# w1 groups in two transfers of 256 KB, a reserve for each transpose in the plan, and a newly drawn order

## The chip, the cores and the metric

The kernel runs on one core of one Trainium2 chip. The metric is the device time of one execution in microseconds (us), the median of several. A core has the engines TensorE (PE, with its weight loads shown apart as PEld), VectorE (DVE), ScalarE (ACT), GpSimd (POOL) and SyncE (SP), which here issues nearly all transfers.

## The reference

A block of a transformer on one sequence of 2048 tokens of width 576, all in bf16. The attention works on four segments of 512 tokens, with 32 heads of 18: causal softmax attention inside a segment, and a memory `M`, `z` of all earlier segments, mixed by a gate per head. The feed-forward part has 4608 hidden units.

```python
def _A_ref(x, wq, wk, wv, wo, beta):
    ...
    phi = lambda t: jnp.where(t > 0, t + 1.0, jnp.exp(t))
    ...
    for s in range(N):                                   # 4 segments of 512
        logits = jnp.einsum('bhqd,bhkd->bhqk', qs, ks) * scale + mask
        p = _softmax(logits, axis=-1)
        a_dot = jnp.einsum('bhqk,bhkd->bhqd', p, vs)
        pq = phi(qs)
        num = jnp.einsum('bhld,bhde->bhle', pq, M)
        den = jnp.einsum('bhld,bhd->bhl', pq, z)[..., None] + 1e-06
        o = g * (num / den) + (1.0 - g) * a_dot
        outs.append(o)
        pk = phi(ks)
        M = M + jnp.einsum('bhld,bhle->bhde', pk, vs)
        z = z + jnp.einsum('bhld->bhd', pk)
    ...
    return o @ wo

def _B_ref(x, w1, b1, w2, b2):
    h = jnp.einsum('bsd,df->bsf', x, w1) + b1
    h = _gelu(h)
    return jnp.einsum('bsf,fd->bsd', h, w2) + b2

h = x + _A_ref(_layernorm(x), A_wq, A_wk, A_wv, A_wo, A_beta)
h2 = h + _B_ref(_layernorm(h), B_w1, B_b1, B_w2, B_b2)
```

## The kernel before

The 2048 tokens are worked on in 8 chunks of 256 (16 tiles of 128). Every chunk goes through these streams:

- **stream_P**: layernorm, the normed tile transposed (`xT`), the projections to q, k and v (L551 and L552, in `mm5`), q and k transposed into `QT` and `KT`. The first chunks transpose on TensorE (L582, L670), the later ones by a DMA transpose (`dma_t`, L323).
- **stream_A**: 80 visits of scores (L752, sixteen small matmuls in tiles of 32 rows, four at a time into `st`), the exponential on ScalarE (L758), the causal mask on GpSimd or VectorE (L763, L765), and the weighted values (L784, into `ox`). From the second segment on, the memory's part (L794 to L814) is added.
- **stream_M**: the memory's sums (L710) for six chunks.
- **stream_B**: the attention's output transposed (by `dma_t` from the second chunk on), the output projection, residual, second layernorm, and its transpose `xn2T`.
- **stream_F1**: the first feed-forward product in 9 groups of 512 hidden units for each chunk, 72 groups in all. Each group needs a fresh copy of its part of w1, in one of up to eight buffers (two of their own, `w1g`, three that lie in `hT` for a while, three in `wqkv` once the projections are done). The width 576 is cut into 4 x 128 rows (`w1_main`, L1061) and 64 left over, the tails. From the second chunk on the tails run as matmuls in tiles of 64 rows (L1048) ahead of the group's others; behind the attention's end up to three groups share one such stretch. The bias is added by VectorE (L1071) or ScalarE (L1069), the gelu by ScalarE (L1083).
- **stream_F2**: the second product (L1110), 36 matmuls for each half of a tile, then the residual from `hd` by way of `hc` (L1099) and the store (L1118, L1120).

The order of all this is not left to the program's text. The kernel contains a planner that plays the execution through with fixed costs: each `op` has an engine, a duration, what it reads and writes, and a due time, which is the plan's clock plus an entry of `SLACK`; `PHASES` replaces entries of `SLACK` at certain times of the plan. Whenever an engine is free, the ready operation with the earliest due time goes first. TensorE takes what the streams offer, with rules for joining a stretch of scores with a stretch of tails (`linger`, `alone`). Where nothing is ready in the beginning, it creates a filler, a matmul on zeros (L1179). A transfer has a `receipt` time beside its bytes (`transfer`, `begin`); its landing frees what waits for it in the plan.

When the plan is done, `arranged` takes each engine's operations in the order of the plan and moves some of them: `MOVES` is a table of pairs for each engine, "operation number i behind operation number j". The numbers are places in the list `ops`, in the order of creation. The result is issued as it stands, each engine in its own order; semaphores hold the data dependencies on the chip. So a plan that errs shows as waits, and the order is not adapted on the chip.

All transfers go through SP's one queue, in the order of the table. Those that the change touches are made in `load_w1` (L974 the main part of 512 KB, L977 twice 32 KB for the tails) and in `dma_t` (L323).

Of the kernel before, what the change touches and what calls it, by code (L numbers as in the profile page):

```python
# [16 lines left out]
def kernel(  # L17
# [16 lines left out]
    P = 128  # L34
# [24 lines left out]
    def sbuf(name, shape, dt=BF16):  # L59
# [8 lines left out]
    NEVER = 1e9  # L68
    TABLE_LOAD = 1.283
    SLACK = dict(zero=19, head=36, lnp=38.5, lnb=53, pow=-202, apply=-44.5, ek_k=497.5, relu_k=102, min_k=61, add_k=34.5,  # L70
                 mz=152.5, exp=-105.5, ek=-79.5, relu=-88.5, min=192.5, add=160, hb=-200.5, gelu=56, finish=35.5, mem=-80,
                 sum=23.5, out=-77.5, hd=122.5, xp=-148, xb=-22.5, t_x=-121.5, t_q=365, t_k=36, t_o=175.5, t_h=161, w1=101,
                 w2=116.5, hc=-15, evict=-236.5, qk=-22.5, ot=126.5, mask=78.5, lead=42.5, balance=254, alone=0, linger=1.5,
                 g=9.5, x1=80, hold=-133.5, ln0=-100)
# [11 lines left out]
                        t_q=338.5, t_h=201, w1=161.5, hc=156.5, qk=-90, ot=27, lead=41.25, balance=118.5, g=90, x1=13, hold=-201.5)),  # L86
              (90, dict(zero=-3, head=133, lnp=103, lnb=42.5, pow=-287, apply=-65.5, ek_k=456, relu_k=25, min_k=-34, add_k=73.5,
# [7 lines left out]
                        balance=117.5, g=86.5, x1=31, hold=-200.5)),  # L95
              (130, dict(lnp=38, lnb=63.5, relu_k=119, min_k=-28, add_k=105, mz=66.5, min=116, add=113.5, gelu=21, finish=17,
# [16 lines left out]
              (240, dict(zero=-55, head=-105.5, lnp=36.5, lnb=91.5, pow=-253.5, apply=23, ek_k=666.5, relu_k=262, min_k=-78.5,  # L113
                        add_k=59, mz=-61.5, exp=2.5, ek=6, relu=-109, min=204.5, add=-49.5, hb=-348, gelu=3.5, finish=3, mem=-13,
                        sum=179, out=-151.5, hd=101.5, xp=-381.5, xb=-36.5, t_x=-116.5, t_q=343.5, t_k=282.5, t_o=180, t_h=235,
                        w1=95.5, w2=120, hc=194.5, evict=-454, qk=-86.5, ot=26, mask=-34, lead=36, balance=190.5, linger=2.5, g=213,
                        x1=34.5, hold=-86.5, ln0=42)),
# [7 lines left out]
              (330, dict(zero=-20, head=-128.5, lnp=11.5, lnb=94.5, pow=-248.5, apply=-19, ek_k=787.5, relu_k=313, min_k=-113.5,  # L125
                        add_k=84.5, mz=-51, exp=74, ek=-71, relu=-139, min=71, add=-38.5, hb=-398.5, gelu=-87, finish=-8.5,
                        mem=-44.5, sum=155.5, out=-124.5, hd=207.5, xp=-331.5, xb=-36.5, t_x=-24.5, t_q=422.5, t_k=139.5, t_o=142,
                        t_h=382.5, w1=123, w2=70.5, hc=13.5, evict=-539.5, qk=-92.5, ot=95, mask=62, lead=34.5, balance=193,
                        alone=4, linger=1, g=359, x1=94, hold=-139, ln0=-106)),
# [7 lines left out]
    MOVES = dict(PE=[74, -1, 71, 73, 77, 71, 81, 78, 75, 81, 85, 75, 89, 80, 93, 89, 86, 82, 90, 84, 83, 88, 97, 83, 94, 97, 102,  # L137
# [30 lines left out]
                                      ACT=[59, 53, 61, 54, 45, 113, 124, 120, 135, 124, 55, 130, 155, 145, 168, 171, 224, 218, 56,  # L168
# [152 lines left out]
    def dma_t(blocks, dst, src, rd, wr, slack=0.0):  # L321

        o = op("SP", 1.25, lambda: nc.sync.dma_start_transpose(out=dst, in_=src), rd, wr, slack)  # L323
        return transfer(o, blocks * 45 + 70, 1.4, rd, wr, 0.2)
# [221 lines left out]
    def mm(n):  # L546
        return n * MM + 0.003
# [710 lines left out]
```

## Time and profile before

| | before |
|---|---|
| runs | 467.14, 467.19, 468.15 us; median 467.19 |
| profiled execution | 467.02 us, of which the span in the profile is 465.1 us |
| granted TensorE clock | 0.999 of full speed |
| busy TensorE / weight loads | 459.2 us / 351.6 us |
| busy VectorE / ScalarE / GpSimd | 272.9 / 320.0 / 180.0 us |
| DMA | 80.89 MB, mean 174 GB/s; the main queue's packets take 69.7% of the 16 DMA engines |
| issued by SP | 393 transfers, 64 of them transposes |

A view by stretches gives, for each stretch of the span, the busy time of each engine with the number of its instructions, then the granted clock and the DMA's share and rate. A row of the waits gives who waited, for whom, the sum, the number of times and the longest, in us; PEld is TensorE's weight load, SPq the queue of SP, and "issue" means that nothing in the profile released it. A timeline row gives start, length, engine, line, operation and tiles, shape and number of instructions; lengths of matmuls overlap with the next row, so starts are compared.

### The profile page before, as it was taken

What the parts mean: (1) busy time and instruction counts of PE and PEld (TensorE: products, weight loads), DVE (VectorE), ACT (ScalarE), POOL (GpSimd) and SP (SyncE); (2) the same over time, 40 slices, a digit from 0 to 9 for tenths busy, and PEclk for the clock granted to TensorE, in tenths of its full rate; (3) what the DMA queues carried; (4) which work ended last, traced back from release to release, by engine and by line L of the source; (5) the groups of instructions that cost most, each with busy time, mean ns of one, the idle gap of its engine ahead of it and who ended that gap; (6) DMA issues with size and microseconds to landing.
All of it is one profiled execution on the core that took longest, in us unless ns stands there. A gap on an engine that the chain in (4) does not pass through costs nothing.

```text
span 465.1 us, 14420 instructions
## 1 busy us (share of the span) xinstructions
PE 459.2 (99%) x6102; PEld 351.6 (76%) x6102; DVE 272.9 (59%) x712; ACT 320.0 (69%) x299; POOL 180.0 (39%) x240
## 2 busy tenths in 40 slices
PE   8999999999999999999999999999999999999997
PEld 6777787777677777767677777678778788888885
DVE  4889878787874355777755647687345524212020
ACT  3987788977888877966768778658778453423620
POOL 4567233778563144487442116474233401000000
PEclk9999999999999999999999999999999999999999
DMA  8889699887598557587876645989956595747211
GB/s 210 251 257 293 127 205 192 177 216 153 130 220 205 167 148 222 129 164 150 152 178 184 176 154 149 169 192 196 229 168 178 167 215 169 155 126 222 68 40 51
DMA packets 123152, 80.89 MB, mean 174 GB/s; under 512 B 57536, under 2 KB 121040, under 8 KB 123088
## 3 DMA queue, kind: packets, MB, share of 16 engines
q1 hardware_dynamic: 123056, 79.98, 69.7%
q8 instruction: 47, 0.77, 0.7%
q0 software_dynamic: 32, 0.01, 0.1%
q14 instruction: 17, 0.14, 0.1%
HBM read 60.03 MB, written 7.08 MB: 144 GB/s over the span
## 4 chain that ended last, share of the span: by engine, by line
PE 96%; DMA 2%; DVE 1%; SPq 0%; issue 0%
PE bank L1110 25%; PE bank L1061 22%; PE bank L551 14%; PE ox L784 7%; PE st L752 6%; PE late L1110 5%; PE late L1061 4%; PE bank L1048 4%; PE bank L552 3%; DMA wqkv<-in_A_wq_dram 2%; PE bank L1021 1%; PE ox L1110 1%; PE bank L807 1%; PE bank L670 1%; PE ox L1061 1%; PE bank L710 1%
## 5 line engine op out<-in xcount | busy, mean ns | idle before, releaser
L758 ACT ACTIVATE pt<-st 128x2048 bf16<-128x2048 f32 x80 | 150.2, 1878 | 56.8 <-PE st L752 51.5
L1110 PE MATMUL bank<-w_sb,hT 128*128 128x288 bf16 x936 | 135.9, 286 | 0.0
L1110 PEld LDWEIGHTS <-hT 128*128 128x128 bf16 x1152 | 109.1, 98 | 26.9 <-issue 1.1
L1071 DVE TENSOR_TENSOR hT<-bank,b1T 128x512 bf16<-128x512 f32 x78 | 53.8, 689 | 69.0 <-PE bank L1061 68.5
L1061 PE MATMUL bank<-xn2T,w1g 128*128 128x256 bf16 x688 | 87.9, 273 | 0.0
L1061 PEld LDWEIGHTS <-w1g 128*128 128x128 bf16 x768 | 70.6, 98 | 16.0 <-issue 6.7
L763 POOL TENSOR_SCALAR_AFFINE_SELECT pt<-pt 128x512 bf16<-128x512 bf16 x84 | 54.1, 657 | 71.2 <-ACT pt L758 66.3
L1083 ACT ACTIVATE hT<-hT 128x1536 bf16<-128x1536 bf16 (+3 forms) x24 | 66.0, 2764 | 16.4 <-DVE hT L1071 16.2
L551 PE MATMUL bank<-wqkv,xT 128*128 128x432 bf16 (+1 forms) x268 | 57.1, 336 | 0.7 <-DMA wqkv<-in_A_wq_dram 0.7
L551 PEld LDWEIGHTS <-xT 128*128 128x128 bf16 x400 | 36.5, 97 | 19.7 <-issue 0.9
L784 PEld LDWEIGHTS <-pt 128*128 128x128 bf16 x1280 | 42.2, 96 | 4.5 <-issue 0.6
L784 PE MATMUL ox<-v_aug,pt 128*128 128x19 bf16 x1280 | 44.1, 172 | 0.0
L752 PE MATMUL st<-QT,KT 32*128 32x128 bf16 x1280 | 32.4, 217 | 0.6 <-issue 0.6
L799 POOL TENSOR_TENSOR pq<-ek,pq 128x512 bf16<-128x512 bf16 x24 | 27.9, 1162 | 12.6 <-DVE ek L797 10.8
L752 PEld LDWEIGHTS <-KT 32*128 32x128 bf16 x1280 | 18.5, 92 | 16.2 <-issue 14.3
L829 POOL TENSOR_TENSOR o_nat<-t,t 128x288 bf16<-128x288 f32 x24 | 19.9, 830 | 25.7 <-DVE t L828 25.6
L1069 ACT ACTIVATE hT<-bank,b1T 128x256 bf16<-128x256 f32 x62 | 25.8, 473 | 5.6 <-PE bank L1061 4.6
L1061 PEld LDWEIGHTS <-wqkv 128*128 128x128 bf16 x272 | 26.0, 98 | 4.5 <-issue 0.4
L1110 PE MATMUL late<-w_sb,hT 128*128 128x288 bf16 x180 | 25.0, 286 | 0.0
L795 POOL TENSOR_SCALAR pq<-QT 128x512 bf16<-128x512 bf16 x24 | 15.4, 641 | 24.7 <-PE bank L807 9.9
L569 POOL TENSOR_TENSOR rstd_b<-rstd_b,mhalf 128x1 f32<-128x1 f32 x16 | 9.6, 602 | 39.2 <-DVE rstd_b L564 39.2
L931 POOL TENSOR_TENSOR h_t<-h_t,b_bc 128x576 f32<-128x576 f32 x16 | 20.7, 1296 | 6.0 <-DVE xn L573 4.8
(136 smaller groups left out, 620.1 us busy)
## 6 DMA issues: line engine op xcount, KB each, us to landing
w1g<-in_B_w_dram SPq DMA_DIRECT2D x50, 512.0 KB, 4.3
wqkv<-in_B_w_dram SPq DMA_DIRECT2D x17, 512.0 KB, 4.1
w_sb<-in_B_w_dram SPq DMA_DIRECT2D x6, 864.0 KB, 6.0
hd<-h_t SPq DMA_DIRECT2D x16, 288.0 KB, 3.0
hc<-hd SPq DMA_DIRECT2D x32, 144.0 KB, 2.8
w1g<-in_B_w_dram SPq DMA_DIRECT2D x100, 32.0 KB, 3.1
x_b<-in_A_x_dram SPq DMA_DIRECT2D x18, 144.0 KB, 3.7
hT<-in_B_w_dram SPq DMA_DIRECT2D x5, 512.0 KB, 5.6
```

The lines of the kernel that those rows point to most:

```text
L551: nc.tensor.matmul(out=out_ap, lhsT=lhsT_of(slice(0, P), k), rhs=rhs_of(slice(0, P), k), start=(k == 0), stop=False)
L752: nc.tensor.matmul(out=st4[:, i, n * P:(n + 1) * P], lhsT=KTs[(c - c % 2 + kt // 2) % 3][rows, g, (kt % 2) * P:(kt % 2 + 1) * P], rhs=QTs[ ...
L758: op("ACT", 1.88, lambda: nc.scalar.activation(out=pt[:], in_=st4[:], func=ACT.Exp, scale=scale), sk, [("pt", slot, n) for n in range(4)], ...
L763: either(("POOL", 0.64, lambda part=part: nc.gpsimd.affine_select(out=part, in_=part, pattern=[[0, 4], [1, P]], compare_op=ALU.is_ge, fill ...
L784: nc.tensor.matmul(out=oxv[:, 4 * (g % 4) + i, :], lhsT=pts[slot][:, i, n * P:(n + 1) * P], rhs=v_augs[(2 * s0 + kt) % 6][:, 4 * g + i, :] ...
L799: op("POOL", 1.16, lambda: nc.gpsimd.tensor_tensor(out=pq[:], in0=e_g, in1=pq[:], op=ALU.add), ["ek"], ["pq"], slack=SLACK["add"])
L931: op("POOL", 1.29, lambda: nc.gpsimd.tensor_tensor(out=h_t[:], in0=h_t[:], in1=b2_bc[:], op=ALU.add), ["b2"], [("h", tl)], slack=SLACK["hb"])
L1061: nc.tensor.matmul(out=banks[b][:, a * Q:(a + 1) * Q], lhsT=w1_main(wt)[:, k, (2 * (h % 2) + a) * P:(2 * (h % 2) + a + 1) * P], rhs=xn2T[c ...
L1069: nc.scalar.activation(out=hT[:, f + a, :], in_=banks[b][:, a * Q:(a + 1) * Q], func=ACT.Identity, bias=b1T[:, f + a:f + a + 1])
L1071: either(("DVE", 0.69, lambda hT=hT, f=f, b=b: nc.vector.tensor_tensor(out=hT[:, f:f + 2, :], in0=banks[b][:].rearrange("p (a w) -> p a w" ...
L1083: op("ACT", (f1 - f0) * Q * 0.00083 + 0.18, lambda hT=hT, f0=f0, f1=f1: nc.scalar.activation(out=hT[:, f0:f1, :], in_=hT[:, f0:f1, :], fun ...
L1110: nc.tensor.matmul(out=acc, lhsT=hT[:, q, tl * P:(tl + 1) * P], rhs=w2_sb[:, q, hs], start=(q == 0), stop=(q == NF - 1))
```

## The change

Four edits. (1) `load_w1` issues the 512 KB of a group as two transfers of 256 KB, each with a key of its own; the matmuls wait for both. The two transfers of 32 KB for the tails stay. (2) In the plan each transpose lands `RESERVE` = 0.6 us later than before; `d.pad` is read nowhere in the kernel. (3) The due times: the base entries of `SLACK` are replaced, two new entries of `PHASES` come in at 50 and 110 us, those at 240 and 330 us are changed in part, the others stay. (4) `MOVES` is another table (TensorE 305 pairs for 295, ScalarE 77 for 68, VectorE 265 for 287, GpSimd 113 for 112, SP 268 for 213). No computation changes.

```diff
+    RESERVE = 0.6
-    SLACK = dict(zero=19, head=36, lnp=38.5, lnb=53, pow=-202, apply=-44.5, ek_k=497.5, relu_k=102, min_k=61, add_k=34.5,
...
+    SLACK = dict(zero=25.5, head=44, lnp=45.5, lnb=75, pow=-181.5, apply=-50, ek_k=548.5, relu_k=99.5, min_k=59.5, add_k=64,
...
+              (50, dict(zero=65, head=49, lnp=67.5, lnb=42, pow=-339, apply=-21.5, ek_k=540, relu_k=61, min_k=-62, add_k=101.5,
...
+              (110, dict(head=78.5, lnp=20.5, min_k=-14.5, add_k=82, mem=-149.5, sum=113.5, out=-68.5, t_q=345.5, w1=129.5, hc=116,
...
     MOVES = dict(PE=[...],
...
-                                      SP=[7, 8, 6, 7, 65, 6, 210, 65, 318, 210, 64, 318, 190, 9, ... 189, 417,
-                      ... 2504, 2492, 2539, 2527])
+                                      SP=[3, 1, 5, 2, 72, 4, 8, 7, 66, 8, 192, 66, 215, 192, 235, 215, 71, 235, 327, 71, 194, 327,
+                      233, 194, 65, 10, 236, 65, 191, 236, 9, 191, 268, 11, 70, 63, 214, 70, 220, 214, 299, 220, 213, 299, 281, 64,
+                      193, 281, ... 2599, 2587, 2611, 2598])
...
     def dma_t(blocks, dst, src, rd, wr, slack=0.0):
 
         o = op("SP", 1.25, lambda: nc.sync.dma_start_transpose(out=dst, in_=src), rd, wr, slack)
-        return transfer(o, blocks * 45 + 70, 1.4, rd, wr, 0.2)
+        d = transfer(o, blocks * 45 + 70, 1.4, rd, wr, 0.2 + RESERVE)
+        d.pad = RESERVE
+        return d
...
-        dma(512, lambda: nc.sync.dma_start(out=w1_main(wt), in_=B_w1[0:512, fcols].rearrange("(k p) f -> p k f", p=P)), (), [k], SLACK["w1"])
+        for h in range(2):
+            dma(256, lambda h=h: nc.sync.dma_start(out=w1_main(wt)[:, 2 * h:2 * h + 2, :],
+                                                   in_=B_w1[256 * h:256 * h + 256, fcols].rearrange("(k p) f -> p k f", p=P)), (), [(*k, "m", h)], SLACK["w1"])
...
-                        wk = [k, (*k, 0), (*k, 1)]
+                        wk = [(*k, 0), (*k, 1), (*k, "m", 0), (*k, "m", 1)]
...
-                wk = [key for _, k in w1s for key in (k, (*k, 0), (*k, 1))]
+                wk = [key for _, k in w1s for key in ((*k, 0), (*k, 1), (*k, "m", 0), (*k, "m", 1))]
...
-                        op("PE", 4 * mm(Q), go, xk + [k], [b], n=8)
+                        op("PE", 4 * mm(Q), go, xk + [(*k, "m", 0), (*k, "m", 1)], [b], n=8)
```

More of the change, by code (lines that the diff above doesn't have):

```diff
@@ L68 @@
     NEVER = 1e9
+    RESERVE = 0.6
     TABLE_LOAD = 1.283
-    SLACK = dict(zero=19, head=36, lnp=38.5, lnb=53, pow=-202, apply=-44.5, ek_k=497.5, relu_k=102, min_k=61, add_k=34.5,
[L71 to L74, printed above, removed]
+    SLACK = dict(zero=25.5, head=44, lnp=45.5, lnb=75, pow=-181.5, apply=-50, ek_k=548.5, relu_k=99.5, min_k=59.5, add_k=64,
+                 mz=214, exp=-121, ek=-80, relu=-54.5, min=168.5, add=162.5, hb=-204, gelu=61.5, finish=-14.5, mem=-108.5,
+                 sum=51, out=-14.5, hd=136.5, xp=-155.5, xb=-8.5, t_x=-147.5, t_q=388.5, t_k=61.5, t_o=174, t_h=190, w1=118,
+                 w2=138, hc=-47, evict=-218.5, qk=-24, ot=127, mask=60.5, lead=41.25, balance=254, alone=0, linger=2.5,
+                 g=3.5, x1=81, hold=-179.5, ln0=-138)
     PHASES = [(30, dict(zero=31.5, head=69.5, lnp=42, pow=-174, apply=-18.5, ek_k=572, relu_k=123, min_k=-8, add_k=97, mz=106.5,
@@ L86 @@
                         t_q=338.5, t_h=201, w1=161.5, hc=156.5, qk=-90, ot=27, lead=41.25, balance=118.5, g=90, x1=13, hold=-201.5)),
+              (50, dict(zero=65, head=49, lnp=67.5, lnb=42, pow=-339, apply=-21.5, ek_k=540, relu_k=61, min_k=-62, add_k=101.5,
+                        mz=109.5, exp=-48, ek=-251, relu=-111.5, min=79.5, add=130, hb=-298, gelu=-28, finish=38, mem=-96, sum=160,
+                        out=-71.5, hd=214.5, xp=-236, xb=15, t_x=-120.5, t_q=375.5, t_k=-43, t_o=146.5, t_h=153.5, w1=145.5, w2=22,
+                        hc=191.5, evict=-362.5, qk=-130.5, ot=68.5, mask=63.5, lead=35.5, balance=104, linger=4, g=73, x1=2.5,
+                        hold=-235, ln0=46.5)),
               (90, dict(zero=-3, head=133, lnp=103, lnb=42.5, pow=-287, apply=-65.5, ek_k=456, relu_k=25, min_k=-34, add_k=73.5,
@@ L95 @@
                         balance=117.5, g=86.5, x1=31, hold=-200.5)),
+              (110, dict(head=78.5, lnp=20.5, min_k=-14.5, add_k=82, mem=-149.5, sum=113.5, out=-68.5, t_q=345.5, w1=129.5, hc=116,
+                        evict=-324, ot=38, balance=117)),
               (130, dict(lnp=38, lnb=63.5, relu_k=119, min_k=-28, add_k=105, mz=66.5, min=116, add=113.5, gelu=21, finish=17,
@@ L112 @@
                         evict=-346.5, qk=-100.5, ot=31, lead=43, balance=141, linger=1, g=138.5, x1=56.5, hold=-173, ln0=-88.5)),
[L113 to L117, printed above, removed]
+              (240, dict(zero=-55, head=-105.5, lnp=36.5, lnb=93.5, pow=-254.5, apply=31, ek_k=666.5, relu_k=264, min_k=-78.5,
+                        add_k=59, mz=-61.5, exp=2.5, ek=4, relu=-107, min=204.5, add=-49.5, hb=-348, gelu=-0.5, finish=-30, mem=-14,
+                        sum=179, out=-167.5, hd=125.5, xp=-413.5, xb=-36.5, t_x=-116.5, t_q=343.5, t_k=282.5, t_o=180, t_h=243,
+                        w1=95.5, w2=119.5, hc=194.5, evict=-454, qk=-86.5, ot=26, mask=-42, lead=37, balance=198.5, linger=2.5,
+                        g=213, x1=30.5, hold=-134.5, ln0=42)),
               (290, dict(zero=-27.5, head=-102.5, lnp=22, lnb=89.5, pow=-245, apply=-23.5, ek_k=777.5, relu_k=282, min_k=-137,
@@ L124 @@
                         hd=174.5, xp=-350.5, xb=-45.5, t_x=-47, t_q=371, t_k=169.5, qk=-84, ot=27, mask=74.5, alone=0.3, ln0=-89)),
[L125 to L129, printed above, removed]
+              (330, dict(zero=-20, head=-162.5, lnp=11.5, lnb=94.5, pow=-248.5, apply=-19, ek_k=787.5, relu_k=313, min_k=-113,
+                        add_k=52.5, mz=-51, exp=70, ek=-103, relu=-139, min=71, add=-42.5, hb=-398.5, gelu=-87, finish=-8.5,
+                        mem=-44.5, sum=155.5, out=-124.5, hd=207.5, xp=-347.5, xb=-36.5, t_x=-24.5, t_q=422.5, t_k=139.5, t_o=142,
+                        t_h=385.5, w1=123, w2=70.5, hc=-18.5, evict=-539.5, qk=-92.5, ot=95, mask=62, lead=34.5, balance=193,
+                        alone=4, linger=0, g=359, x1=95.5, hold=-124, ln0=-106)),
               (360, dict(zero=-34, lnp=5.5, lnb=93.5, pow=-238, ek_k=659, relu_k=282.5, min_k=-9, mz=-118.5, exp=-35, ek=17,
```

9 lines of the change are left out of this document (4 added, 5 removed), and 200 rows, old and new, of tables (ACT, DVE, MOVES, POOL).

## The prediction

> **What bounds the kernel now.** I read the profile's page first, then busy times by stretch, then the waits of TensorE and of its weight loads, then its timeline.
>
> ```profile
> PE 459.2 (99%) x6102; PEld 351.6 (76%) x6102; DVE 272.9 (59%) x712; ACT 320.0 (69%) x299; POOL 180.0 (39%) x240
> PE 96%; DMA 2%; DVE 1%; SPq 0%; issue 0%
> ...
> 0.00:23.00 23.00, 21.08 (x236) 16.44 (x237) 15.73 (x57) 14.88 (x22) 12.04 (x24) 1.00 0.84 229
> 23.00:90.00 67.00, 66.23 (x1163) 50.29 (x1162) 57.09 (x151) 55.76 (x45) 32.21 (x44) 1.00 0.89 214
> 90.00:372.00 282.00, 281.98 (x3915) 211.78 (x3913) 178.47 (x466) 215.35 (x189) 133.33 (x171) 1.00 0.72 174
> 372.00:462.00 90.00, 89.95 (x796) 73.05 (x793) 21.16 (x41) 34.03 (x45) 2.41 (x3) 1.00 0.51 135
> 462.00:465.20 3.20, 0.00 (x0) 0.00 (x0) 0.45 (x1) 0.00 (x0) 0.00 (x0) 0.84 0.08 23
> ```
>
> TensorE is busy 459.2 us of 465.1, and 96% of the chain that ended last is TensorE. The stretches show where the other 5.9 us are: 1.9 in the first 23 us, 0.8 up to 90 us, 0.1 in the 372 us after that, 3.2 behind the last matmul. The granted clock is 1.00 wherever matmuls run. From 90 us on no wait is left to be removed. What TensorE waited for, in total, times and the longest in us:
>
> ```profile
> PE ox L1179 <- DVE pq L508: 1.3, 1, 1.3
> PE bank L551 <- DMA wqkv<-in_A_wq_dram: 0.7, 1, 0.7
> PE st L752 <- issue: 0.6, 1, 0.6
> ...
> PEld L752 <- issue: 14.3, 55, 0.8
> PEld L1061 <- issue: 7.6, 36, 0.2
> PEld L1048 <- issue: 4.9, 20, 0.4
> ...
> PEld L551 <- DMA xT<-o_nat: 0.2, 1, 0.2
> PEld L1061 <- DMA QT<-qk_pad: 0.2, 1, 0.2
> PEld L1061 <- DMA w1g<-in_B_w_dram: 0.2, 1, 0.2
> ```
>
> Two of the three waits of the matmuls are the start of the kernel (constants, the first weights). In the whole run the weight loads waited once for a w1 transfer and twice for a transpose, 0.2 us each. These are the transfers that the change deals with, so little can come back from them. But "busy" still hides something: 14.3 + 7.6 + 4.9 = 26.8 us of "issue" before the weight loads of three lines, those where the array changes between tiles of 32 rows (scores, L752), of 64 rows (the tails of F1, L1048) and whole ones. The timeline gives the price:
>
> ```profile
> 138.75 0.55 PE L784 MATMUL ox<-v_aug,pt 128*128 128x19 bf16 x16
> 139.24 0.40 PE L752 MATMUL st<-QT,KT 32*128 32x128 bf16 x16
> 139.57 0.39 PE L1048 MATMUL bank<-xn2T,w1g 64*128 64x256 bf16 x4
> 139.90 1.05 PE L1061 MATMUL bank<-xn2T,w1g 128*128 128x256 bf16 x8
> ...
> 141.06 0.55 PE L784 MATMUL ox<-v_aug,pt 128*128 128x19 bf16 x16
> 141.46 1.03 PE L1061 MATMUL bank<-xn2T,w1g 128*128 128x256 bf16 x8
> 142.33 0.44 PE L710 MATMUL bank<-v_aug,phik_pad 128*128 128x76 bf16 x8
> 142.61 1.14 PE L1110 MATMUL bank<-w_sb,hT 128*128 128x288 bf16 x8
> 143.68 0.40 PE L752 MATMUL st<-QT,KT 32*128 32x128 bf16 x16
> ...
> L752 PEld LDWEIGHTS <-KT x1280: 90/93/94, 15.1 to 366.5; 32*128 32x128 bf16 x183
> ...
> L1048 PEld LDWEIGHTS <-w1g x192: 92/94/96, 71.5 to 436.7; 64*128 64x128 bf16 x192
> ```
>
> Sixteen matmuls of L784 take 141.46 - 141.06 = 0.40 us before whole tiles and 139.24 - 138.75 = 0.49 before scores: a change of tiling costs 0.09 us. At 139.24 scores and tails stand side by side, three changes instead of four. Counted through the whole timeline, from 15.1 to 436.7 us, there are 80 stretches of scores (1280 / 16) and 55 of tails, 40 of the 55 with a score beside them: 2 x (80 + 55) - 40 = 230 changes, about 21 us. At best all 55 are joined, which takes 15 changes away: 1.4 us.
>
> [...]
>
> **The change, part by part.** The sum is made on the profiled execution: 467.02 us, of which 465.1 are its span; the median of the three runs is 467.19, 0.17 more.
>
> ```profile
> w1g<-in_B_w_dram SPq DMA_DIRECT2D x50, 512.0 KB, 4.3
> wqkv<-in_B_w_dram SPq DMA_DIRECT2D x17, 512.0 KB, 4.1
> ...
> hd<-h_t SPq DMA_DIRECT2D x16, 288.0 KB, 3.0
> hc<-hd SPq DMA_DIRECT2D x32, 144.0 KB, 2.8
> ...
> hT<-in_B_w_dram SPq DMA_DIRECT2D x5, 512.0 KB, 5.6
> ...
> L974 SPq DMA_DIRECT2D w1g<-in_B_w_dram x50: 372/498/1672, 16.1 to 424.3; - x50
> ...
> L323 SPq DMA_TRANSPOSE xT<-o_nat x14: 1204/1212/1846, 55.3 to 372.6; - x14
> ...
> L323 SPq DMA_TRANSPOSE KT<-qk_pad x12: 1241/1276/2548, 63.7 to 329.6; - x12
> ...
> DMA to landing us min/median/max: 2.6/3.6/5.8
> ```
>
> Two transfers for one. There are 50 + 17 + 5 = 72 loads, so 72 transfers are added, at 0.5 us of SP's time each: 36 us. SP issues in order, so what stands behind a second half is 0.5 us later: often a transpose, or the two small tails of the same group. A half should land 2.8 to 3.0 us after its issue (between the rows for 144 and 288 KB), and the second half, issued 0.5 us behind the first, in 3.3 to 3.5, against 4.3 for the whole. A wait of TensorE becomes two, on transfers that land one behind the other; its price, where the data are there, is zero up to the 0.05 us of a semaphore instruction (row below), 55 times, hence 0 to 2.8 us:
>
> ```profile
> L1048 PEldq EVENT_SEMAPHORE  x7: 51/51/51, 93.5 to 407.0; - x7
> ```
>
> I take zero, since at 139.57 the tails follow 0.33 us behind scores, just as L1061 follows the tails, although they already wait for three transfers. A gain is bounded by the one 0.2 us wait.
>
> [...]
>
> The reserve. Each of the 64 transposes (14 + 14 + 12 + 12 + 12 in five groups, the first and the last of them above) counts as landed 0.6 us later in the plan; the chip does nothing more for it. Where a reader would have stood at once behind the landing, other work goes in first. Cover: other streams have matmuls ready (281.98 busy of 282.00). Without cover it would cost 64 x 0.6 = 38 us. I take zero for it, and -0.3 for what it removes: two waits of 0.2 us, less what comes up elsewhere. It also covers the 0.5 us that SP is later.
>
> Due times and moves. This is the part with no row of its own: another order of the same matmuls. The diff bounds it. The numbers in the table are places in the list of operations as the plan makes them. SP's largest goes from 2539 to 2611, by 72, just the added transfers; the first w1 load behind the start begins at 189 before, and SP's numbers 191 to 194 can only be that load after: two more operations ahead of it, those of the first two groups. So the new plan very likely has the same fillers and the same groups of tails, and TensorE's work is the same:
>
> ```profile
> L1179 PE MATMUL bank<-pq 128*128 128x256 bf16 x43 | 9.1, 338 | 0.0
> L1179 PE MATMUL ox<-pq 128*128 128x256 bf16 x10 | 3.3, 372 | 1.3 <-DVE pq L508 1.3
> ```
>
> These 53 fillers stand where nothing is ready, all in the first 23 us; their number shows how much of the start is dependence. Left to the order are the changes of tiling: 5 more or fewer (a third of the 15) make 0.45 us either way; I take 0, as nothing in the diff says which way. The 3.2 us behind the last matmul are an eviction and a store and stay.
>
> Sum: 467.0 + 0 (split) - 0.3 (waits) + 0 (order) = 466.7 for a profiled execution, and with the 0.17 above, 466.9 for the median.
>
> **The rivals.** First, the new order is shorter. All 15 joins (1.4), the 0.6 us of "issue" in L752 and the 0.3 from above make 2.3 us, 464.9; two thirds of that, 1.5, give 465.7. For it: 26.8 us of changes is the only reserve in the trace, and the due times that decide on them are all new. Against it: a gain of over 0.2% (0.93 us, about what a measurement of this kernel can tell from no change) needs some ten joins, or seven and a wait, out of fifteen.
>
> Second, slower: an order drawn up in a plan meets transfers and engines that are not where the plan has them. The place is SP's queue between 90 and 372 us. There the transposes alone hold SP for 64 x 1.2 = 77 us, the 72 w1 loads with their two small tails for 72 x 3 x 0.5 = 108, and 144 after. One load that waits for its buffer holds up all behind it:
>
> ```profile
> SPq L974 <- PE bank L1061: 22.4, 17, 3.4
> ```
>
> A transpose behind such a wait (1.3 us on average, 3.4 at most) is late by 0.5 us more than now, and TensorE, which takes its own order as written, stands until it lands. With the wait's 1.3 us, less the reserve, a stall is about 0.7 us: two make it slower, three cost 2.1 us, 469.0. For it: three transfers already land in the moment of their use (the waits of 0.2), so that the margins are near zero at places. Against it: the reserve is larger than the 0.5 us.
>
> Third, the reserve and the split do nothing, and the order comes out alike: 467.2, inside my forecast.
>
> **How the numbers follow.** No change beyond 0.2% (466.9, own range 466.3 to 468.1): 0.37, with the third rival in it. Shorter order: 0.30. Stalls: 0.33. For an 80% range I leave out 0.09 below 465.2 (nearly all joins) and 0.10 above 469.2 (more than three stalls). The range is mostly that of the stalls, whose number no row gives.
>
> **What would show it.** Right: TensorE's busy time within 1 us of 459.2, 53 fillers, the "issue" rows of L752, L1061 and L1048 together within 0.5 us of 26.8, no DMA behind a wait of PE or PEld above 0.3 us, 144 w1 transfers of 256 KB landing in 3 to 3.5 us. The first rival shows in the "issue" rows (down by over 1 us) at the same number of matmuls; the second in the stretches 90:372 and 372:462, with TensorE's busy time under 281 or 89 us and a transpose, a w1 load or a softmax tile as releaser. The forecast is wrong if the number of fillers differs, for then the start was planned anew, which I excluded, or if the time behind the last matmul does.

## The result and the profile after

The changed kernel takes 473.93 us (median of four runs, 472.12 to 476.30) against 467.44 for the kernel before beside it (467.14 to 468.15): a ratio of 1.0143 with a 95% interval of 1.0118 to 1.0168, slower by 6.7 us. The prediction said 466.9 us in 465.2 to 469.2. The profiled execution took 472.75 us, of which 471.0 are its span, 5.9 more than before.

The page of the profile after, its busy times and the chain that ended last, by engine and then by line:

```profile
PE 461.6 (98%) x6102; PEld 353.6 (75%) x6102; DVE 257.2 (55%) x689; ACT 322.4 (68%) x318; POOL 183.8 (39%) x247
PE 94%; DMA 3%; ACT 1%; DVE 0%; issue 0%; SPq 0%; ACTq 0%
```

TensorE's matmuls are the same in number, 6102, but it is busy 2.4 us longer, and DMA has gone from 2% to 3% of the chain. The view by stretches of the kernel after says where:

```profile
0.00:23.00 23.00, 21.66 (x265) 17.04 (x266) 17.68 (x62) 15.16 (x22) 12.71 (x25) 1.00 0.89 254
23.00:90.00 67.00, 65.17 (x1165) 49.91 (x1164) 54.51 (x148) 55.46 (x48) 37.18 (x53) 0.97 0.82 206
90.00:372.00 282.00, 278.89 (x3832) 208.52 (x3829) 164.52 (x440) 208.73 (x189) 130.83 (x168) 0.99 0.73 169
372.00:462.00 90.00, 90.00 (x802) 73.72 (x800) 19.56 (x38) 43.08 (x62) 3.06 (x3) 1.00 0.51 148
```

The start is a little better filled (21.66 against 21.08). Between 23 and 372 us two things are new: TensorE stands 1.8 and 3.1 us, where it stood 0.8 and 0.02, and the granted clock, the column behind the five engines, is 0.97 and 0.99 where it was 1.00. The waits of TensorE and of its weight loads (sum, times, longest):

```profile
PE bank L564 <- DMA wqkv<-in_B_w_dram: 3.1, 2, 2.8
PE bank L1194 <- DVE pq L521: 1.3, 1, 1.3
PE st L765 <- ACT pt L771: 1.3, 1, 1.3
...
PEld L765 <- issue: 13.4, 51, 1.2
PEld L1076 <- issue: 7.6, 36, 0.2
PEld L1063 <- issue: 5.0, 21, 0.2
```

The constants (1.3 us) were there before. New are 3.1 us in which the projections to q, k and v (L564) wait for a load of w1, and 1.3 us in which a stretch of scores (L765) waits for an exponential; two more waits are of 0.4 and 0.2 us. The three rows of "issue", the changes of tiling, stand as they did.

**The wait for w1 at 299 us.** Before, the weights of q, k and v are overwritten by w1 only once the last projection is done. The loads of w1 into `wqkv` between 280 and 325 us before, then between 240 and 325 us after, with the first and last start:

```profile
L974 SPq DMA_DIRECT2D wqkv<-in_B_w_dram x3: 577/578/763, 314.2 to 318.9; - x3
```

```profile
L988 SPq DMA_DIRECT2D wqkv<-in_B_w_dram x5: 416/476/572, 249.0 to 315.6; - x5
```

After, the first is issued 65 us sooner, and four of the five before or among the last chunk's projections. SP's queue and TensorE's timeline around the last two of these four (start, length; in brackets the idle time and who ended it):

```profile
290.99 0.42 SPq L988 DMA_DIRECT2D wqkv<-in_B_w_dram  x1
294.93 1.21 SPq L334 DMA_TRANSPOSE xT<-xn  x1
...
298.92 0.52 SPq L988 DMA_DIRECT2D wqkv<-in_B_w_dram  x1
```

```profile
295.56 0.52 PE L564 MATMUL bank<-wqkv,xT 128*128 128x432 bf16 x2 [0.26 <-DMA wqkv<-in_B_w_dram]
...
297.99 0.90 PE L564 MATMUL bank<-wqkv,xT 128*128 128x432 bf16 x4
298.74 0.35 PE L565 MATMUL bank<-wqkv,xT 65*128 65x432 bf16 x1
301.93 1.62 PE L564 MATMUL bank<-wqkv,xT 128*128 128x432 bf16 x4 [2.84 <-DMA wqkv<-in_B_w_dram]
```

The load at 298.92 is written into the projections' weights, and the projections that come next in the order wait until it has landed: 2.84 us. The reason is in the code. The planner tracks what may be overwritten by keys; when the projections are done, `more_w1` gives the three buffers in `wqkv` the projections as readers, under these keys:

```python
for k in (("w1q", j), ("w1q", j, 0), ("w1q", j, 1)):
    readers[k] = list(readers["wqkv_pad"])
```

The change gives the two halves the keys `(*k, "m", 0)` and `(*k, "m", 1)`, which are not in this list. So in the plan the halves wait for no projection, and the new table has four pairs that use it: SP 1957 behind 1578, 1965 behind 1757, 1962 behind 1988 and 1958 behind 1869.

This costs more than time. By the code, buffer j in `wqkv` begins at column 2304 j of the 8640 columns in which the weights of q, k and v lie as five blocks of 1728. The four halves are issued ahead of the last chunk's projections or in the midst of them (294.8 to 309.7 us), and the first, 1957, takes columns 0 to 1023 of the first block: the first 128 rows of q's weights and of most of k's. The last chunk's projections multiply by w1 there. So the words "No computation changes" do not hold for this chunk.

**The clock.** The row of L564 at 301.93 has a second half to it: four matmuls take 1.62 us there and 0.90 at 297.99. Stretches of the kernel after, around both new waits; the granted clock, as a share of full speed, is the column behind POOL:

```profile
45.47:48.88 3.41, 2.15 (x70) 2.01 (x68) 2.47 (x7) 3.06 (x3) 1.45 (x3) 1.00 0.93 283
48.88:52.29 3.41, 3.41 (x62) 3.18 (x59) 2.06 (x7) 1.69 (x3) 0.00 (x0) 0.50 0.31 105
298.70:301.90 3.20, 0.38 (x3) 0.00 (x0) 1.27 (x3) 1.53 (x1) 2.81 (x4) 0.93 0.74 230
301.90:304.85 2.95, 2.92 (x9) 1.23 (x10) 0.84 (x3) 0.50 (x2) 0.00 (x0) 0.50 1.02 227
304.85:310.00 5.15, 5.15 (x66) 3.12 (x65) 2.45 (x8) 3.63 (x6) 0.89 (x2) 1.00 0.44 104
```

With each of the two stalls the clock is 0.50 here for 3.41 us, from 48.88 to 52.29 us and, beginning 0.46 us before TensorE goes on, from 301.47 to 304.88. TensorE is busy 3.41 and 2.96 us of that; about half of it, 1.7 and 1.5 us, is lost (an estimate from the clock) and counts as busy. That is the main reason why the busy time has grown. The stretch from 290 to 310 us, before and then after:

```profile
290.00:310.00 20.00, 20.00 (x247) 13.66 (x248) 14.86 (x39) 12.85 (x13) 11.62 (x15) 1.00 0.86 171
```

```profile
290.00:310.00 20.00, 16.89 (x175) 10.33 (x172) 9.73 (x30) 12.59 (x15) 8.21 (x12) 0.91 0.66 155
```

3.1 us idle and 0.09 x 20 = 1.8 us of clock make 4.9 us. Counted more closely, from the starts of all matmuls (the time to the next start, beyond what the same pair takes elsewhere), it is 4.8 us from 290 to 310 us, 1.6 from 40 to 60 (the scores' stall and the half clock behind it, beyond the 0.8 us that TensorE stands there before), 0.8 in small pauses from 70 to 90, 0.5 for five more changes of tiling, and 1.6 less in the start: 6.1 in all, against the span's 5.9.

**The scores' wait at 46 us.** In the new order two stretches of scores stand close together (timeline of the kernel after):

```profile
45.08 0.40 PE L765 MATMUL st<-QT,KT 32*128 32x128 bf16 x16
45.41 0.56 PE L797 MATMUL ox<-v_aug,pt 128*128 128x19 bf16 x16
45.83 0.43 PE L723 MATMUL bank<-v_aug,phik_pad 128*128 128x76 bf16 x8
47.52 0.41 PE L765 MATMUL st<-QT,KT 32*128 32x128 bf16 x16 [1.25 <-ACT pt L771]
```

An exponential takes 1.88 us (L771, 80 of them in 150.2 us), and between the two scores lies work for only 0.9 us; the second waits for `st`, which the first one's exponential still reads.

### The profile page after: what moved, and what is told of

Its sections match the earlier page's. It is cut to its first block, busy times and chain, and to the rows that moved or that the text cites. A ratio compares the mean times of both kernels' runs of the same rounds, so it can differ in the third digit from the quotient of the medians.

```text
span 471.0 us, 14516 instructions
## 1 busy us (share of the span) xinstructions
PE 461.6 (98%) x6102; PEld 353.6 (75%) x6102; DVE 257.2 (55%) x689; ACT 322.4 (68%) x318; POOL 183.8 (39%) x247
## 4 chain that ended last, share of the span: by engine, by line
PE 94%; DMA 3%; ACT 1%; DVE 0%; issue 0%; SPq 0%; ACTq 0%
PE bank L1125 26%; PE bank L1076 18%; PE bank L564 13%; PE ox L797 7%; PE st L765 5%; PE late L1076 5%; PE late L1125 4%; PE bank L565 3%; PE bank L1063 3%; PE bank L1036 2%; DMA wqkv<-in_B_w_dram 2%; PE ox L1076 1%; PE bank L1194 1%; DMA xT<-xn 1%; PE bank L820 1%; PE bank L723 1%
## 5 line engine op out<-in xcount | busy, mean ns | idle before, releaser
L771 ACT ACTIVATE pt<-st 128x2048 bf16<-128x2048 f32 x80 | 150.2, 1877 | 50.1 <-PE st L765 48.4
L1125 PE MATMUL bank<-w_sb,hT 128*128 128x288 bf16 x1008 | 145.3, 286 | 0.0
L1076 PE MATMUL bank<-xn2T,w1g 128*128 128x256 bf16 x680 | 86.0, 273 | 0.0
L776 POOL TENSOR_SCALAR_AFFINE_SELECT pt<-pt 128x512 bf16<-128x512 bf16 x91 | 59.0, 662 | 69.0 <-ACT pt L771 61.3
L1076 PEld LDWEIGHTS <-w1g 128*128 128x128 bf16 x784 | 73.1, 98 | 16.5 <-issue 6.7
L1086 DVE TENSOR_TENSOR hT<-bank,b1T 128x512 bf16<-128x512 f32 x69 | 47.4, 690 | 50.3 <-PE bank L1076 50.1
L564 PE MATMUL bank<-wqkv,xT 128*128 128x432 bf16 (+1 forms) x268 | 58.6, 342 | 3.5 <-DMA wqkv<-in_B_w_dram 3.1
L564 PEld LDWEIGHTS <-xT 128*128 128x128 bf16 x400 | 36.2, 98 | 24.8 <-DMA wqkv<-in_B_w_dram 3.3
L1129 DVE TENSOR_TENSOR ot<-bank,hc 128x288 bf16<-128x288 f32 x28 | 12.7, 455 | 49.6 <-PE bank L1125 33.3
L765 PE MATMUL st<-QT,KT 32*128 32x128 bf16 x1280 | 32.4, 218 | 1.3 <-ACT pt L771 1.3
L1084 ACT ACTIVATE hT<-late,b1T 128x256 bf16<-128x256 f32 x32 | 13.0, 474 | 28.3 <-PE late L1076 28.2
L765 PEld LDWEIGHTS <-KT 32*128 32x128 bf16 x1280 | 18.8, 93 | 15.6 <-issue 13.4
L644 ACT CAST qk_pad<-bank 128x432 bf16<-128x432 f32 (+1 forms) x30 | 13.9, 466 | 20.9 <-PE bank L565 16.4
L565 PE MATMUL bank<-wqkv,xT 65*128 65x432 bf16 (+1 forms) x67 | 22.9, 341 | 0.0
```

The source lines that it names most:

```text
L564: nc.tensor.matmul(out=out_ap, lhsT=lhsT_of(slice(0, P), k), rhs=rhs_of(slice(0, P), k), start=(k == 0), stop=False)
L565: nc.tensor.matmul(out=out_ap, lhsT=lhsT_of(slice(0, KTAIL), 4), rhs=rhs_of(slice(0, KTAIL), 4), start=False, stop=True)
L765: nc.tensor.matmul(out=st4[:, i, n * P:(n + 1) * P], lhsT=KTs[(c - c % 2 + kt // 2) % 3][rows, g, (kt % 2) * P:(kt % 2 + 1) * P], rhs=QTs[ ...
L771: op("ACT", 1.88, lambda: nc.scalar.activation(out=pt[:], in_=st4[:], func=ACT.Exp, scale=scale), sk, [("pt", slot, n) for n in range(4)], ...
L776: either(("POOL", 0.64, lambda part=part: nc.gpsimd.affine_select(out=part, in_=part, pattern=[[0, 4], [1, P]], compare_op=ALU.is_ge, fill ...
L1076: nc.tensor.matmul(out=banks[b][:, a * Q:(a + 1) * Q], lhsT=w1_main(wt)[:, k, (2 * (h % 2) + a) * P:(2 * (h % 2) + a + 1) * P], rhs=xn2T[c ...
```

## The experiments

Each kernel was run against the kernel before; ratios are to that, with 95% intervals. 0.1% is 0.47 us.

### The changed kernel once more

No edit.

> The changed kernel once more, unchanged. The first profile of it has TensorE standing 0.3 + 2.8 us between 295 and 302 us for transfers of w1 into the buffers that lie in wqkv, 1.25 us at 46.2 us for a softmax tile, and two stretches of 3.41 us at half the granted clock (48.9 and 301.5 us). If these stalls are fixed by the written order, they come back at the same places and the time is again 472 to 476 us. If they were the chance of one execution, the stalls stand elsewhere.

474.91 us, 1.0143 [1.0109, 1.0177]. The projections' wait for w1 (3.2 us) and the scores' wait (1.3 us) are there again, so both belong to the order and not to one execution. At 46 us the clock stayed at 1.00 (rows in the last section). Over the span it is 0.992, about what two stretches of 3.41 us at half clock take off the mean (an estimate: 3.41 of 471.7 us). Of the eight runs of this kernel on record one has a granted clock of 1.00 and took 472.12 us; the seven others have 0.988 to 0.993 and took 472.75 to 476.30. So the half clock is not the whole of the loss.

### The keys guarded, the four early loads put back (e1)

```diff
-    for k in (("w1q", j), ("w1q", j, 0), ("w1q", j, 1)):
+    for k in (("w1q", j), ("w1q", j, 0), ("w1q", j, 1), ("w1q", j, "m", 0), ("w1q", j, "m", 1)):
...
+    sp = [list(p) for p in zip(MOVES["SP"][0::2], MOVES["SP"][1::2]) if p[0] not in (1957, 1958, 1962, 1965)]
+    MOVES["SP"] = [n for i, after in sp for n in (i, 1869 if after == 1958 else after)]
```

> The changed kernel, but the two new keys of each buffer in wqkv wait for the last reader of wqkv in the plan, as the old key did, and the four w1 halves that the table put ahead of the last chunk's projections stay at their planned place. Theory A (these halves make the projections wait and halve the clock afterwards): the stall near 298 us and the slow stretch behind it are gone, 4.8 us less, about 468 to 470 us. Theory B (SP's queue is late because of the 72 added transfers): under 1 us less, the stalls move to transposes nearby. Theory C (the new order is longer in itself): under 2 us less.

471.13 us, 1.0073 [1.0043, 1.0103]. No load stands behind a wait of the projections any more, and half of the loss is gone: 0.0143 - 0.0073 = 0.0070 (±0.0039), 3.3 us. The profiled execution of this kernel shows a wait that the changed kernel did not have:

```profile
PE st L767 <- DMA QT<-qk_pad: 2.4, 1, 2.4
PE bank L1065 <- DVE ot L1131: 1.5, 1, 1.5
PE st L767 <- ACT pt L773: 1.3, 1, 1.3
```

### The same early loads in the kernel before (e8)

Two whole loads into `wqkv` lose their predecessors and go ahead of the last projections, in the order of before. The last chunk's projections read w1 in part there.

```diff
+        for i, after in ((1893, 1732), (1896, 1827)):
+            ops[i].preds = []
+            line["SP"].remove(ops[i])
+            line["SP"].insert(line["SP"].index(ops[after]) + 1, ops[i])
```

> The kernel before, with two of the three 512 KB loads into wqkv issued behind transposes of the last chunk, ahead of that chunk's projections, which then wait for them and read w1 in those columns. Theory A: one or two waits of 2 to 4 us of TensorE near 295 to 302 us, each with up to 3.4 us at half clock behind it: 3 to 7 us slower than before, 471 to 475 us. If the waits were not the cause, within 1 us of before.

476.02 us, 1.0200 [1.0172, 1.0229], 9.3 us slower, more than either expectation had. The waits of TensorE and the pieces of the chain (start, length) in this kernel:

```profile
PE bank L551 <- DMA wqkv<-in_B_w_dram: 6.5, 2, 4.2
```

```profile
291.13 5.35 DMA wqkv<-in_B_w_dram
...
304.38 3.96 DMA wqkv<-in_B_w_dram
```

So two such loads are enough, without split, reserve or new order. Whole ones, 512 KB each, made TensorE wait longer here than the halves did, 6.5 us against 3.1.

### The split alone, in the order of before (e2)

```diff
+        def halves():
+            for h in range(2):
+                nc.sync.dma_start(out=w1_main(wt)[:, 2 * h:2 * h + 2, :],
+                                  in_=B_w1[256 * h:256 * h + 256, fcols].rearrange("(k p) f -> p k f", p=P))
...
-        dma(512, lambda: nc.sync.dma_start(out=w1_main(wt), ...
+        dma(512, halves, (), [k], SLACK["w1"])
```

> The kernel before with its own plan, due times and moves; only, each w1 load is issued as two transfers of 256 KB one behind the other at the place of the one. Theory A: within 0.5 us of before, 467 to 468 us, with no new wait of TensorE over 0.3 us. Theory B: 2 to 6 us slower, with transposes and w1 tiles as releasers between 90 and 372 us.

469.25 us, 1.0026 [1.0003, 1.0049]: 1.2 us slower, with an interval that reaches almost to nothing. Where TensorE waited once 0.2 us for a transpose before, it now waits once 1.1 us (`xT<-o_nat`), and once 0.8 us for `ot`.

### Whole loads in the new order with the keys guarded (e4)

e1, with one transfer of 512 KB at the place of the first of the two issued halves; the second issues nothing.

```diff
+        def whole(h):
+            if h == 0:
+                nc.sync.dma_start(out=w1_main(wt), in_=B_w1[0:512, fcols].rearrange("(k p) f -> p k f", p=P))
...
+            dma(256, lambda h=h: whole(h), (), [(*k, "m", h)], SLACK["w1"])
```

> As e1_guard, but each w1 group is again one transfer of 512 KB, issued at the place of the first half; nothing at the place of the second. Theory A: the same time as e1_guard within 1 us. Theory B: 2 us or more faster than e1_guard. Theory C: same as A.

469.75 us, 1.0034 [1.0012, 1.0055]. Against e1 the whole loads gain 0.0039 (±0.0037), 1.8 us; the wait for QT is not there, but one for w1 is:

```profile
PE bank L1081 <- DMA w1g<-in_B_w_dram: 2.2, 1, 2.2
```

By the granted clock of each run, 9 of e1's 12 runs are at 0.996 or less and 5 of e4's; one stretch of 3.41 us at half clock takes the mean to 0.996 (an estimate: 1.7 of 470 us). The others are not apart: 468.32 to 469.30 us in e1 (three runs), 467.71 to 470.14 in e4 (seven). So the 1.8 us show in how often the clock was that low; that few runs do not tell more. The new order without the split is still 1.6 us slower than that of before.

### e4 with the two scores set apart (e5)

```diff
+        for i, after in ((375, 372), (379, 381), (383, 379)):
+            line["PE"].remove(ops[i])
+            line["PE"].insert(line["PE"].index(ops[after]) + 1, ops[i])
```

> As e4_guard_whole (4 early loads held back, one transfer of 512 KB: 469.75 us), and three operations of TensorE put elsewhere near 45 us, so that some 2 us of other matmuls lie between two stretches of scores that now have 0.8 us between them; the second of them waits 1.26 us for the exponential of the first. If this wait is what the new order costs, 1.3 us less, and up to 1.7 more where a stretch at half clock followed it: 467.0 to 468.5 us. If the order is longer all over, under 0.5 us less.

467.90 us, 1.0012 [0.9997, 1.0027]. With whole loads and both faults taken out, the reserve and the new order together are worth what the old order was. The step from e4 is 0.0022 (±0.0026): about 1 us, not told from none by the times. The profiled execution of this kernel ran at a granted clock of 0.755, so no stretch of it is read here.

### The split put back into the mended order (e12)

e5 with the two halves instead of the whole load:

```diff
-            dma(256, lambda h=h: whole(h), (), [(*k, "m", h)], SLACK["w1"])
+            dma(256, lambda h=h: nc.sync.dma_start(out=w1_main(wt)[:, 2 * h:2 * h + 2, :],
+                                                   in_=B_w1[256 * h:256 * h + 256, fcols].rearrange("(k p) f -> p k f", p=P)), (), [(*k, "m", h)], SLACK["w1"])
```

> The changed kernel with the four early loads held back and the scores near 45 us set apart, but with two transfers of 256 KB for each group: e5_scores_apart (467.9 us) with the split back in. If the causes add up, e5's time and the split's 1.2 to 1.5 us: 469.1 to 469.4 us. If the split costs nothing in an order without other faults, 467.5 to 468.3 us.

471.65 us, 1.0086 [1.0056, 1.0117]: the miss is 2 us. In this order the split costs 0.0074 (±0.0034), 3.5 us, not the 1.2 of e2. And against e1 no gain of the scores set apart shows (0.0013 ± 0.0043 slower). The largest wait of TensorE, beside 1.6 us in two waits for w1, is:

```profile
79.42 0.40 PE L767 MATMUL st<-QT,KT 32*128 32x128 bf16 x16 [2.42 <-DMA QT<-qk_pad]
```

```profile
70.83 1.61 SPq L990 DMA_DIRECT2D hT<-in_B_w_dram  x3
72.50 1.24 SPq L336 DMA_TRANSPOSE QT<-qk_pad  x1
```

TensorE arrives at these scores at 77.0 us, and their QT, issued behind three halves into `hT`, is there only at 79.4. In e1 the same scores wait as long and begin at 80.12 us, so that 0.7 us of the gain at 46 us is left behind this wait in these two executions; that the rest is lost at this transpose was a theory, which the next run tries.

### QT ahead of the three halves (e13)

```diff
+        line["SP"].remove(ops[497])
+        line["SP"].insert(line["SP"].index(ops[498]) + 1, ops[497])
```

> The mended order with halves (keys guarded, early loads put back, scores apart; 1.0086 [1.0056, 1.0117]) and one more move in SP's order: the transpose of QT that was issued at 72.5 us goes ahead of the three halves of w1 into hT. Theory A (what is gained before 77 us is waited for at that transpose, 2.4 us): the wait for QT is gone and the ratio falls by 0.003 to 0.005, to 1.004 to 1.006. Theory B (the split costs at many places, by SP's time): another wait of about 2 us comes in its place and the ratio stays within 0.002 of 1.0086.

469.80 us, 1.0045 [1.0026, 1.0063]: 0.0041 (±0.0036) less than e12, the first theory's 0.003 to 0.005. The transpose goes out at 68.33 and the scores follow the matmuls ahead of them without a wait (SP's queue and TensorE's timeline):

```profile
68.33 2.01 SPq L336 DMA_TRANSPOSE QT<-qk_pad  x1
70.39 1.61 SPq L990 DMA_DIRECT2D hT<-in_B_w_dram  x3
```

```profile
76.03 0.40 PE L767 MATMUL st<-QT,KT 32*128 32x128 bf16 x16
```

So, by the medians, about half of the split's price in this order was one transpose behind three halves; a new wait of 1.4 us for VectorE (`t`, before the tails) stands in the profile of e13. What is left against e5, 0.0033 (±0.0024), is near the price in e2.

### The changed kernel with only the scores set apart (e14)

The three moves of e5, in the changed kernel as it is:

```diff
+        for i, after in ((375, 372), (379, 381), (383, 379)):
+            line["PE"].remove(ops[i])
+            line["PE"].insert(line["PE"].index(ops[after]) + 1, ops[i])
```

> The changed kernel with the two scores at 46 us set apart and nothing else (the last chunk's projections read w1 in part, as in the changed kernel itself). Theory A (the gain is handed on to the transpose of QT): the wait for the exponential is below 0.5 us, a wait for QT of 1 to 2.5 us appears at 75 to 80 us, and the time falls by 0 to 0.9 us, ratio 1.0125 to 1.0143. Theory B (the terms add): 1.6 us less, ratio 1.0105 to 1.0115, and no wait for QT.

472.73 us, 1.0121 [1.0084, 1.0157]: 1.0 us less than the changed kernel, between the two expectations, and the interval of the difference (±0.0044) holds both. The wait for QT did not come in the profiled execution, the fastest of the six (469.64 us, at a clock of 1.00), which speaks against the first theory in this kernel. The profile keeps the larger fault:

```profile
PE bank L564 <- DMA wqkv<-in_B_w_dram: 2.9, 2, 2.5
...
PE st L765 <- ACT pt L771: 0.4, 1, 0.4
```

### One load sooner in e5 (e15)

```diff
+        line["SP"].remove(ops[1953])
+        line["SP"].insert(line["SP"].index(ops[1968]) + 1, ops[1953])
```

> The mended order with whole loads (1.0012 [0.9997, 1.0027]) and one load of w1 into w1g, at 321 us, put ahead of two transposes (315 to 317 us), since TensorE waited 2.2 us for it at 325 us in the same order without the scores apart. If that wait is paid in full: 0.9965 to 0.998, faster than before. If the wait only moves to the transposes behind it or is absent in this version: 1.000 to 1.002.

469.64 us, 1.0040 [1.0019, 1.0061], slower than e5, which neither expectation had. Of the wait for w1 that e4 has at 325 to 327 us, 0.3 us is left, and close to that place, up to 324.7 us, the tails wait 2.0 us for VectorE:

```profile
PE bank L1068 <- DVE ot L1134: 2.0, 1, 2.0
```

It was not followed why `ot` is late there. No version tried beats the kernel before.

### A tiny transfer behind each w1 load (e6), the two tails as one (e7)

Both in the order of before: 72 transfers of 512 bytes more (e6), 72 of 64 KB in place of 144 of 32 KB (e7).

```diff
+            nc.sync.dma_start(out=tiny[16 * n:16 * n + 16, :], in_=B_w1[0:16, 0:16])
```

```diff
+            if h == 0:
+                nc.sync.dma_start(out=wt[:, 4 * 512:W1], in_=B_w1[512:576, fcols].rearrange("p (h f) -> h p f", h=2))
```

> The kernel before, with one tiny transfer (512 bytes, to a place that nobody reads) issued behind each of the 72 w1 transfers of 512 KB, which stay whole. It costs SP's time like the split, without cutting anything. If the split's 1.2 to 1.5 us are SP being 0.5 us later at each load, the same 1.2 to 1.5 us: 469 us. If they come from the smaller transfers themselves, within 0.5 us of before.

> The kernel before, with the two transfers of 32 KB of each group issued as one of 64 KB at the place of the first: 72 issues fewer on SP. If SP's time is what counts, waits get fewer and the time is 0.3 to 1 us under before; if before has its transfers in time anyway, the same within 0.3 us. A loss would mean that the one transfer, issued at the place of the first or of the other, lands too late for its readers.

Both missed. e6: 472.71 us, 1.0104 [1.0081, 1.0128], 4.9 us for as many issues as the split adds at 1.2 us, though a half of 256 KB moves so much more. By the code the tiny transfers write to a DRAM tile (`tiny`), which the halves do not; whether that matters was not tried. e7: 472.32 us, 1.0107 [1.0069, 1.0144], slower although SP issues 72 transfers fewer. So neither measures SP's 0.5 us by itself, and how the split's remaining price of about 1.2 us divides into SP's time and the landing stays open.

### Without the tables of moves (e9, e10, e11)

```diff
+    MOVES = {e: [] for e in MOVES}
```

```diff
-        return transfer(o, blocks * 45 + 70, 1.4, rd, wr, 0.2)
+        return transfer(o, blocks * 45 + 70, 1.4, rd, wr, 0.2 + 0.6)
```

e9 is the kernel before without its table; e10 is e9 with 0.6 us of reserve for each transpose (the second edit) and the due times of before; e11 is the changed kernel without its table.

> The kernel before with its table of moves emptied: the order is the plan's own. It tells what the table is worth: if it only closes small gaps, 1 to 3 us slower than before; if it is what removes the waits for transfers, 5 us or more, with transposes and w1 tiles as releasers of TensorE.

> As e9_before_plain, and in addition the reserve of 0.6 us for each transpose in the plan, with the due times of before. If the reserve does what it says, TensorE's waits for transposes fall against e9_before_plain, by 1 us or more in all, and the time with them. If the plan only shuffles, the same time within 1 us, with waits elsewhere.

> The changed kernel with its table of moves emptied: reserve, two halves and the new due times are in it, and the four halves into wqkv stand behind the projections, where the plan has them. If the new due times are the better ones, it is faster than e9_before_plain by 1 us or more; if only the new table was at fault, about as fast as e9_before_plain; if the due times are worse, slower.

e9: 473.72 us, 1.0132 [1.0111, 1.0153]; e10: 486.51 us, 1.0412 [1.0390, 1.0434]; e11: 474.76 us, 1.0164 [1.0139, 1.0188]. In e9 TensorE waits for transposes:

```profile
PE bank L552 <- DMA xT<-o_nat: 2.9, 5, 0.8
...
PE bank L552 <- DMA xT<-xn: 1.1, 2, 0.8
```

The reserve does take these waits away in e10, but for 0.3 us, and yet 13 us are lost: TensorE now waits 2.8 us for w1, 2.5 for `hT` and 2.1 for `pt`, and the granted clock is 0.989 over the span, about what three stretches of 3.41 us at half clock take off (an estimate: 5.1 of 485.6 us). That due times fit the plan that they were drawn up on, and not a plan with a reserve, is the likely reason; it was not tried by itself. The new due times of e11, which has the split in it too, win that back and no more. The table before is worth 0.0132 to e9. The new one takes e11 only from 1.0164 to 1.0143, and with its two faults out and whole loads to 1.0012.

## Why the prediction was wrong

**The step that failed** is "due times and moves", taken as another order of the same matmuls, whose only cost is changes of tiling. What it said of fillers and matmuls held: 53 fillers, 6102 matmuls. The tails stand in 53 stretches instead of 55; the changes are 235 instead of 230, 0.45 us, the size that the prediction gave to five more. But an order has more in it than tiling: it holds two waits, one for a load (2.84 us) and one for an exponential (1.25 us). The first could be read from the code, and e1, which takes it away, wins back 3.3 (±1.8) of the 6.7 us. The prediction followed the new keys to the matmuls that read them and not to the list in `more_w1` that protects their buffer. Taken out one after the other, the early loads give back 3.3 us (e1), whole loads 1.8 (±1.7, e4) and the scores about 1 (±1.2, e5), and what is left, 0.6 us, is not told from none. They do not simply add: with the split in place the scores give back nothing that shows (e12). The early loads are shown both ways, by e1 and e8; how the rest divides is open.

**The sign** was the second rival's, at 0.33, but not by its mechanism. It had transposes held up behind a waiting load in SP's queue. The 2.84 us are TensorE waiting for the load itself. The transpose behind the load of 290.99 does go out late, at 294.93, but VectorE had finished its `xn` only at 294.90. A transpose that is late behind loads shows elsewhere: that of QT, in e12, behind three halves. The rival's price, 0.7 us for a stall, was too low by more than the wait: a stall here was 1.25 to 2.84 us long, and the half clock behind it added about 1.7 or 1.5 (an estimate from the clock of 0.50). So two stalls cost 4.8 and 1.6 us in the profiled execution, what nine were to cost, and the range, which ended at "more than three stalls" or 469.2, was left by 4.7 us. That such a stall slows TensorE afterwards had no row before: its one pause in mid-work, 0.6 us at 43 us, was followed by a clock of 1.00.

**The split**, taken at zero between 0 and 2.8, costs 1.2 us in the order of before, inside its bounds, and 3.5 in the mended order, beyond them. The landing times were forecast nearly right:

```profile
w1g<-in_B_w_dram SPq DMA_DIRECT2D x102, 256.0 KB, 3.3
wqkv<-in_B_w_dram SPq DMA_DIRECT2D x32, 256.0 KB, 3.7
hT<-in_B_w_dram SPq DMA_DIRECT2D x10, 256.0 KB, 4.4
```

against 3 to 3.5: the 32 into `wqkv` and the ten into `hT` took longer. What failed is the choice of zero: it was argued from tails that already wait for three transfers, which shows that a wait for three of them cost nothing at 139.57 us (0.33 us behind the scores, as much as from the tails to L1061), not that a transpose half a microsecond later costs nothing. That part was named in the second rival and not put into the sum.

**The reserve**, at zero and a gain of 0.3: no run has it alone in an order that fits it. In e10 the waits for transposes are gone and the kernel is 13 us slower; e5, which has it, is not told from before (0.9997 to 1.0027). So the 0.3 us cannot be told from zero.

**The 3.2 us** behind the last matmul stayed, 471.0 - 467.9. Of the signs named, TensorE's busy time (461.6, outside 459.2 ± 1) and a DMA behind a wait of PE above 0.3 us (3.1) showed the forecast wrong; "issue" in the three rows is 26.0 against 26.8, a little outside its 0.5.

## What to carry to other kernels

When a change renames a key, a tag or a semaphore, follow the old name to every place where it is read or protected, those that the diff does not touch above all; a table of moves on a plan with a missing dependency can use the hole, as four pairs did here, and then the result changes as well as the time. Price a stall of TensorE with the slow stretch that can follow it (here 3.41 us at a clock of 0.50 with two stalls, none with two others), and look for it in the column of the granted clock, because it counts as busy (3.41 of 3.41 us behind the first). A gain early in an order can be lost at the next transfer that lands only at its use, as 0.7 us was in e12, where TensorE waited 2.42 us for QT: after mending one place, look at the waits behind it before counting the gain.

## What the runs showed of the hardware

In the profiled execution of the changed kernel half clock came with two pauses, each shorter than the stretch of 3.41 us at half clock. After a wait of 1.25 us (46.27 to 47.52) the clock was 0.50 from 48.88 to 52.29 us; in one of 2.84 us (299.09 to 301.93) it fell to 0.50 at 301.47 and stayed there to 304.88. Half clock does not come with every such pause: with the wait of 1.3 us in the second profiled execution of the changed kernel, and with that of 2.5 us in e14, the clock stayed at 1.00. In the first execution TensorE was busy 2.15 of the 3.41 us ahead of the first stretch at half clock, and 1.02 of the 3.41 us ahead of the second. In the second execution the wait of 1.3 us lies in these two stretches:

```profile
44.63:48.04 3.41, 2.88 (x72) 2.64 (x70) 3.34 (x10) 2.42 (x2) 2.34 (x4) 1.00 0.76 185
48.04:51.46 3.42, 2.69 (x77) 2.56 (x80) 2.47 (x6) 3.19 (x4) 0.88 (x1) 1.00 0.89 284
```

In e14, from 298.70 to 302.00, TensorE was busy 2.01 of 3.30 us and the clock stayed at 1.00, at a share of 0.61 against the 0.63 of 2.15 in 3.41 us. What decides was not tried.

The kernel before itself varied from 465.86 to 470.71 us over the four sets of runs, with medians of 467.11 to 467.71, so that differences of a microsecond need a dozen runs, and several steps here stay inside their intervals. Four of its 80 runs there have a granted clock of 0.996 themselves and took 469.25 to 470.71 us: a part of the scatter between runs goes with a lower granted clock.
